# Attention with a gated expert layer: logits issued ahead of VectorE's reads of the scores, in 32-column tiles, and outputs transposed by halves

## The chip, the core and the metric

The kernel runs on one core of a Trainium2 chip. The metric is the device time of one execution in microseconds (us). Five engines work side by side, each through its own instructions in a fixed order: TensorE (PE in the profile; PEld is its loading of the stationary operand), VectorE (DVE), ScalarE (ACT), GpSimd (POOL) and SyncE (SP), which issues nearly all DMAs.

## The reference, cut to what matters

```python
# q, k, v: (4 batches, 8 heads, 768 positions, 64)
scores = q @ k.T / 8 - slope[head] * distance      # kept: first 8 keys, and the last 96 up to the query
a = softmax(scores over the kept keys)
x = (a @ v), heads side by side                    # 3072 tokens x 512
logits = x @ w_gate                                # 3072 x 8
e = argmax(logits); g = softmax(logits)[e]
# per expert: the 80 tokens with the largest g
out[tok] = g[tok] * (relu(x[tok] @ w1[e]) @ w2[e])  # w1: 512 x 1024, w2: 1024 x 512; all other rows 0
```

Everything is float32.

## The kernel before

The work is in three stages. **Attention** takes 24 blocks of 128 queries, each in two steps of four heads, so 48 steps u = 0 to 47; u // 2 is the block t. **Selection** ranks the tokens of every expert by their gate and makes lists of 80. **Experts** gathers the listed tokens and runs the two layers of eight experts, 512 KB of weights ("quarters") at a time.

In attention the order of work is the order in which the code is written (a manual schedule, all five engines), and each engine goes through its part of it in that order, waiting where it must. One step u issues:

- `transposes(u - 2, u - 5)`: TensorE turns the exponentials of step u - 2 (tiles `pwz`, two 64-row halves at a time, lines 152 and 161) and the attention output of step u - 5 (tile `x`, line 166: two full 128x128 transposes) into the PSUM tiles `tp0` and `tp1`; ScalarE copies `tp0` and VectorE `tp1` into the tile `ta` (lines 170 and 171);
- `scores(u)`: 12 TensorE products (24 records) into the PSUM tile `sc` (line 117; two buffers, two banks each), then four VectorE passes over `sc` that add the bias and find the row's extreme (line 124), each followed by a ScalarE exponential into `pwz` (line 128);
- `logits(u - 6)`: two products of the transposed output with the gate's weights `wgn` (line 215), written into spare columns of the same tile `sc`, and a small VectorE operation that takes them (lines 223 and 225);
- `norm(u - 1)`, and `weigh(u - 3)`: the products with the values `va` and `vb` into the PSUM tile `ub` (lines 187 and 197), and the division by the sum on VectorE (line 203), whose result is `x`; with the second half of a block `x` goes to DRAM;
- some steps of the routing of earlier blocks (`routes(3)`), and the loads of later blocks: SyncE issues q, keys and values four steps ahead, and every third step a quarter of the weights.

The two lines around which the change turns are, in `scores` and in the loop,

```python
                            out=ts[:, j, :w], in0=sc[:, hh, pp, :w], ...   # VectorE reads sc, four times
...
                scores(u)
                if 6 <= u:
                    logits(u - 6)          # TensorE writes the same tile sc
```

In this order TensorE may write the logits into `sc` only after VectorE's reads of `sc`.

After step 47, `DRAIN` lists what is left (t: transposes, l: logits, w: weigh, r and c: routing). Selection has `busy`, dummy products, between its rounds; `WARM` says how many. `NW` is the number of weight buffers in three pools.

Of the kernel before, what the change touches and what calls it, by code (L numbers as in the profile page):

```python
# [10 lines left out]
F32 = mybir.dt.float32  # L11
# [3 lines left out]
ALU = mybir.AluOpType  # L15
AX = mybir.AxisListType
# [14 lines left out]
CR = WH - CA  # L31
CAP = 80
KB = NG + P
NW = (24, 5, 1)
CL = 64

QUARTERS = [(k, e, c) for m in range(E + 1) for k, e in ((1, m), (2, m - 1)) if 0 <= e < E for c in range(4)]
GROUPS = (6, 6, 6, 4, 2)
# [8 lines left out]


DRAIN = (
    "t46,43 l42 w45 r r t47,44 l43 r w46 r r w47 t,45,46 r l44 r r l45 l46 t,47 r r r l47 c r r c r c r c r r c c r"  # L50
)
WARM = (6, 0, 6, 0, 6, 0, 6, 0, 9, 5)
FAR = 1.0e6
END = object()
SLOPES = [2.0 ** -(h + 1) for h in range(H)]
# [2 lines left out]
def fast_path(tc, a, out, cst, x_dram, inp):  # L58
    nc = tc.nc
    V, A, G, T = nc.vector, nc.scalar, nc.gpsimd, nc.tensor  # L60
    ident = cst["ident"]

    with ExitStack() as ctx:
# [20 lines left out]
        with tc.tile_pool(name="at_sb", bufs=2) as sp, tc.tile_pool(name="ps_a", bufs=1, space=PSUM) as psa, ExitStack() as pctx:  # L84

            pwz = [sp.tile([P, 4 * WH + P - CA], F32, name=f"pwz{i}", bufs=1) for i in range(3)]
            st = {}
# [8 lines left out]
            def scores(u):  # L96
                t, g = divmod(u, 2)
                m = TURN[t] % NB
                q, kt = inp.blk[t][0], inp.kts[TURN[t] // NB]
                nm, z, ts, pw = st[u]  # L100
                w = WH if m else P
                st["sc"] = psa.tile([P, 2, 512], F32, tag="sc", bufs=2, name=f"sc{u}")
                sc = st["sc"][:, :, :2 * WH].rearrange("p h (q k) -> p h q k", q=2)

                for pp in range(2):
                    pr = 2 * g + pp
                    for i in range(2):
                        c0 = KB * m - PREV + 64 * i if m else NG
                        for hh in range(2):
                            h = slice(64 * hh, 64 * hh + 64)  # L110

                            cuts = (0, w)
                            if m and i == hh:
                                cuts = (CR, w, 0, CR) if i == 0 else (CA, w, 0, CA)
                            o = 0
                            for c, e in zip(cuts[::2], cuts[1::2]):
                                T.matmul(  # L117
                                    sc[64 * i:64 * i + 64, hh, pp, o:o + e - c], q[h, pr * P + 64 * i:pr * P + 64 * i + 64],
                                    kt[h, pr, c0 + c:c0 + e], start=True, stop=True, skip_group_check=True)
                                o += e - c  # L120
                for hh in range(2):
                    for pp in range(2):
                        j = 2 * pp + hh
                        V.tensor_tensor_reduce(  # L124
                            out=ts[:, j, :w], in0=sc[:, hh, pp, :w], in1=cst["tab" if m else "tab0"][:, 2 * g + pp, hh, :], scale=-0.125,
                            scalar=3.0e38, op0=ALU.add, op1=ALU.min, accum_out=nm[:, j:j + 1],
                        )
                        A.activation(  # L128
                            out=pw[:, j, :w], in_=ts[:, j, :w], func=AF.Exp, bias=nm[:, j:j + 1], scale=-1.0, accum_out=z[:, j:j + 1],
                        )  # L130

            def norm(u):
                z = st[u][1]
# [3 lines left out]
            def transposes(u=None, *xs):  # L137
# [5 lines left out]
                ta = sp.tile([P, 2, 512], F32, tag="ta", name=f"ta{u}_{xs}")  # L143
                hs = [slice(64 * i, 64 * i + 64) for i in range(2)]
                n = 0
                if u is not None:
                    pw = pwz[u % 3]
                    for j in range(4):

                        o = j * WH + (CR if m and j % 2 else 0)  # L150
                        for i in range(2):
                            T.transpose(out=tps[i][:, 64 * j:64 * j + 64], in_=pw[hs[i], o:o + P], identity=ident[hs[i], hs[i]])
                    n = 256
                    st[u, "ta"] = ta
                    if m:
# [53 lines left out]
            def logits(u):  # L209

                t, g = divmod(u, 2)
                ps = st["sc"][:, 1, 2 * WH:2 * WH + E] if g else st["sc"][:, 1, 2 * WH + E:2 * WH + 2 * E]
                xt = st.pop((u, "xt"))
                for pp in range(2):
                    T.matmul(ps, xt[:, pp, :], cst["wgn"][:, 2 * g + pp, :E], start=pp == 0, stop=pp == 1, skip_group_check=True)
                k = next(i for i in range(len(GROUPS)) if t < sum(GROUPS[:i + 1]))
                n, t0 = GROUPS[k], sum(GROUPS[:k])
                if t == t0 and g == 0:
                    st["rt"] = Route(nc, sp, cst, t0, n)
                rt = st["rt"]  # L220
                lg = rt.lg[:, t - t0, :]
                if g == 0:
                    V.tensor_copy(out=lg, in_=ps)
                    return
                V.tensor_tensor(out=lg, in0=ps, in1=lg, op=ALU.add)
                st.pop((t, "x"))
                if n < 3:
                    rt.one(lg, t - t0)
                elif t == t0 + n - 1:
                    routing.append(rt.all())  # L230
                if t == t0 + n - 1 and t < NT - 1:
                    routing.append(rt.rest(lambda: st["sc"][:, 0, 2 * WH:2 * WH + E], cst["capm"]))

            def go(g, n):
                for _ in islice(g, n):
# [7 lines left out]
            routing = []  # L243
# [8 lines left out]
            for u in range(nu):  # L252
# [40 lines left out]

            for _ in islice(wipe, 4):
                pass
            st["sc"] = psa.tile([P, 2, 512], F32, tag="sc", bufs=2, name="rest")
            for k in DRAIN.split():
                if k == "r":
                    routes(1)
                elif k == "c":  # L300
                    go(choice, 1)
                elif k[0] == "t":
                    transposes(*(int(x) if x else None for x in k[1:].split(",")))
                elif k[0] == "w":
                    weigh(int(k[1:]))
                else:
                    logits(int(k[1:]))
                    if k == "l46":
# [6 lines left out]
            go(choice, 99)  # L315
            routes(99)
            assert not routing
            cn = st["sc"][:, 0, 2 * WH:2 * WH + E]
# [777 lines left out]
```

## Time and profile before

| | us |
|---|---|
| median of 3 runs (lowest to highest) | 446.76 (443.24 to 449.04) |
| the profiled execution, its own time | 450.29 |
| its span, first to last instruction | 448.5 |

Columns and terms: a row of a timeline gives the start and the length of an instruction or of a merged run (x24: 24 of them), the line of the kernel, the operation, and in brackets how long the engine had been idle before it and what ended that. Lengths of matmuls are modelled and overlap, so the pace is read from the starts. [...]

### The profile page before, as it was taken

What the parts mean: (1) busy time and instruction counts of PE and PEld (TensorE: products, weight loads), DVE (VectorE), ACT (ScalarE), POOL (GpSimd) and SP (SyncE); (2) the same over time, 40 slices, a digit from 0 to 9 for tenths busy, and PEclk for the clock granted to TensorE, in tenths of its full rate; (3) what the DMA queues carried; (4) which work ended last, traced back from release to release, by engine and by line L of the source; (5) the groups of instructions that cost most, each with busy time, mean ns of one, the idle gap of its engine ahead of it and who ended that gap; (6) DMA issues with size and microseconds to landing.
All of it is one profiled execution on the core that took longest, in us unless ns stands there. A gap on an engine that the chain in (4) does not pass through costs nothing. (4 is left out here: it accounts for less than half of the span.)

```text
span 448.5 us, 12361 instructions
## 1 busy us (share of the span) xinstructions
PE 373.6 (83%) x5149; PEld 275.2 (61%) x5149; DVE 156.2 (35%) x747; ACT 130.8 (29%) x476; POOL 54.6 (12%) x183
## 2 busy tenths in 40 slices
PE   3987877778788777787887877988987999999992
PEld 3766766667666666676666766776443455565551
DVE  5733333454443444434333335335551111001110
ACT  4734234343323334324234233221000211111110
POOL 4200111000002000000200000010207001111112
PEclk9955555555555656555555555555568999999997
DMA  7992135464212446423222430077995999960000
GB/s 208 315 344 78 37 102 162 140 213 140 70 60 89 153 140 213 138 91 109 77 90 91 137 119 26 24 260 288 359 359 144 345 330 364 387 245 25 18 18 24
DMA packets 37812, 73.24 MB, mean 163 GB/s; under 512 B 3476, under 2 KB 10516, under 8 KB 37748
## 3 DMA queue, kind: packets, MB, share of 16 engines
q1 hardware_dynamic: 36452, 69.74, 45.3%
q0 software_dynamic: 1152, 2.63, 1.9%
q8 instruction: 42, 0.69, 0.6%
q14 instruction: 22, 0.18, 0.1%
q10 hardware_dynamic: 144, 0.00, 0.0%
HBM read 58.46 MB, written 14.16 MB: 162 GB/s over the span
## 5 line engine op out<-in xcount | busy, mean ns | idle before, releaser
L128 ACT ACTIVATE pwz<-ts,nm 128x168 f32<-128x168 f32 (+1 forms) x192 | 80.0, 417 | 61.8 <-DVE nm L124 61.7
L117 PE MATMUL sc<-kt,q 64*64 64x104 f32 (+3 forms) x1088 | 65.2, 399 | 6.2 <-DVE kt L858 5.6
L117 PEld LDWEIGHTS sc<-kt,q 64*64 64x64 f32 x1088 | 52.2, 208 | 20.2 <-issue 18.4
L124 DVE CUSTOM_DVE_ANT_0 ts<-sc,tab 128x168 f32<-128x168 f32 (+1 forms) x192 | 51.0, 322 | 30.8 <-PE sc L117 30.7
L203 DVE TENSOR_TENSOR x<-ub,z 128x256 f32<-128x256 f32 x48 | 20.3, 423 | 60.7 <-PE ub L197 56.1
L569 PE MATMUL yp<-w,htm 128*32 128x256 f32 x512 | 39.7, 382 | 1.0 <-DVE vb L614 1.0
L134 POOL TENSOR_SCALAR z<-z 128x4 f32<-128x4 f32 x48 | 10.7, 222 | 241.5 <-ACT pwz L128 241.2
L128 ACT ACTIVATION_READ_ACCUMULATOR pwz<-ts,nm 128x1 f32 x192 | 35.8, 186 | 0.0
L569 PE MATMUL hm<-w,xt 128*32 128x512 f32 x256 | 34.6, 608 | 0.6 <-issue 0.6
L572 PE MATMUL yp<-w,htl 128*32 128x128 f32 x512 | 25.7, 273 | 0.0
L616 POOL DMA_INDIRECT out_dram<-vb,si x16 | 15.6, 975 | 82.4 <-ACT vb L613 39.1
L572 PEld LDWEIGHTS yp<-w,htl 128*32 128x32 f32 x512 | 16.7, 110 | 10.9
L572 PEld LDWEIGHTS hl<-w,xt 128*32 128x32 f32 x256 | 9.1, 112 | 19.2 <-issue 16.9
L572 PE MATMUL hl<-w,xt 128*32 128x256 f32 x256 | 20.7, 390 | 0.0
L585 DVE TENSOR_SCALAR va<-hl 128x256 f32<-128x256 f32 x8 | 3.4, 424 | 39.7 <-PE hl L572 39.7
L425 PE MATMUL lps<-svx,ones 128*128 128x480 bf16 x45 | 16.5, 531 | 0.0
L569 PEld LDWEIGHTS yp<-w,htm 128*32 128x32 f32 x512 | 14.2, 110 | 3.1 <-DVE vb L614 1.2
L124 DVE DVE_READ_ACCUMULATOR2_ANT nm<- 128x1 f32 x192 | 15.9, 83 | 0.0
L561 ACT COPY xt<-xf 128x320 f32<-128x320 f32 x8 | 3.4, 425 | 38.9 <-PE xf L560 32.6
L584 ACT ACTIVATE va<-hm 128x512 f32<-128x512 f32 x8 | 4.8, 597 | 28.5 <-PE hm L569 27.8
L595 DVE COPY htl<-tl 128x256 f32<-128x256 f32 x8 | 3.4, 425 | 26.9 <-PE tl L593 26.9
L614 DVE TENSOR_SCALAR vb<-yp,gs 128x128 f32<-128x128 f32 x8 | 2.8, 350 | 25.9 <-ACT vb L613 25.9
(1051 smaller groups left out, 678.4 us busy)
## 6 DMA issues: line engine op xcount, KB each, us to landing
w<-in_w_dram SPq DMA_DIRECT2D x64, 512.0 KB
x_dram<-x SPq DMA_DIRECT2D x24, 256.0 KB
out_dram<-zero SPq DMA_DIRECT2D x12, 512.0 KB
q<-in_q_dram SPq DMA_DIRECT2D x23, 256.0 KB
vb<-in_vb_dram SPq DMA_DIRECT2D x20, 256.0 KB
va<-in_va_dram SPq DMA_DIRECT2D x20, 208.0 KB
kt<-in_kT_dram SPq DMA_DIRECT2D x4, 816.0 KB
kt<-in_kT_dram SPq DMA_DIRECT2D x3, 544.0 KB
```

The costliest lines, as they stand in the source:

```text
L117: T.matmul(sc[64 * i:64 * i + 64, hh, pp, o:o + e - c], q[h, pr * P + 64 * i:pr * P + 64 * i + 64], kt[h, pr, c0 + c:c0 + e], start=True, ...
L124: V.tensor_tensor_reduce(out=ts[:, j, :w], in0=sc[:, hh, pp, :w], in1=cst["tab" if m else "tab0"][:, 2 * g + pp, hh, :], scale=-0.125, sca ...
L128: A.activation(out=pw[:, j, :w], in_=ts[:, j, :w], func=AF.Exp, bias=nm[:, j:j + 1], scale=-1.0, accum_out=z[:, j:j + 1],)
L134: G.tensor_scalar(out=z, in0=z, scalar1=1.0e-9, scalar2=None, op0=ALU.add)
L203: V.tensor_tensor(out=x[:, 256 * g:256 * g + 256].rearrange("p (q h d) -> p h q d", q=2, h=2), in0=up, in1=z.rearrange("p (q h) -> p h q", ...
L425: nc.tensor.matmul(ps[:, :480], cst["ones"], cst["svx"].rearrange("p s t -> p (s t)"), start=True, stop=True, skip_group_check=True)
L561: A.copy(out=xts[e % 2][:, :, :CAP], in_=xp)
L569: T.matmul(main[p, :n], x[:, 32 * g:32 * g + 32], w[:, n * i:n * i + n], start=first, stop=last, skip_group_check=True)
L572: T.matmul(rest[32 * i:32 * i + 32, :n], xl, w[:, n * i:n * i + n], start=first and rest.tensor is not main.tensor, stop=last, skip_group_ ...
L584: A.activation(out=hs[0], in_=hm, func=AF.Relu)
L585: V.tensor_scalar(out=hs[1], in0=hl[:, :256], scalar1=0.0, scalar2=None, op0=ALU.max)
L616: G.indirect_dma_start(out=out.rearrange("t (q d) -> (t q) d", d=n), out_offset=bass.IndirectOffsetOnAxis(ap=si[:, i, e:e + 1], axis=0), i ...
```

## The change

- `logits` is split by blocks. `logits1(t)`, in odd steps from u = 7, multiplies all of a block's transposed output with the gate's weights: four products, one for each 128 features, each with the 32 columns of `wgn` as the stationary operand, so that each writes 32 rows of its own (a 32-column tile of the array). `take1` copies the 128x128 result to SBUF (`ls`). In the next step `logits2(t)` transposes it back (128x128) and `take2` adds the four parts. Both TensorE parts stand between the score products and VectorE's passes over `sc`; the VectorE parts stand behind the passes.
- The output `x` is transposed in 64-row halves: four products with 64 moving columns for two with 128.
- `ta` has three buffers for two, `ls` is new; the first pool of weights has 23 buffers for 24; `busy` runs 5 products for 6 in four rounds; `DRAIN` is written anew, and its logits of blocks 22 and 23 (`last_logits`) use 64-row output halves.

```diff
-NW = (24, 5, 1)
+NW = (23, 5, 1)
-    "t46,43 l42 w45 r r t47,44 l43 r w46 r r w47 t,45,46 r l44 r r l45 l46 t,47 r r r l47 c r r c r c r c r r c c r"
+    "t46,43 k20 w45 r r t47,44 j21 w46 r r k21 w47 t,45,46 r r l44 l45 r t,47 r r l46 r r l47 c r r c r c r c r r c c r"
-WARM = (6, 0, 6, 0, 6, 0, 6, 0, 9, 5)
+WARM = (5, 0, 5, 0, 5, 0, 5, 0, 9, 5)
...
+                t1, t2 = (u - 7) // 2, (u - 8) // 2
+                if u % 2 and t1 >= 0:
+                    logits1(t1)
+                if u % 2 == 0 and t2 >= 0:
+                    logits2(t2)
                 for hh in range(2):
                     for pp in range(2):
...
+                if u % 2 and t1 >= 0:
+                    take1(t1)
+                if u % 2 == 0 and t2 >= 0:
+                    take2(t2)
...
-                    o = x % 2 * 256
-                    for i in range(2):
-                        T.transpose(
-                            out=tps[i][:, n:n + P], in_=st[x // 2, "x"][:, o + P * i:o + P * i + P], identity=ident)
-                    st[x, "xt"] = ta[:, :, n:n + P]
-                    n += P
+                    for pp in range(2):
+                        o = x % 2 * 256 + P * pp
+                        for i in range(2):
+                            T.transpose(
+                                out=tps[i][:, n:n + 64], in_=st[x // 2, "x"][hs[i], o:o + P], identity=ident[hs[i], hs[i]])
+                        st[x, pp] = ta[:, :, n:n + 64]
+                        n += 64
...
+            def logits1(t):
+
+                for pr in range(NP):
+                    T.matmul(
+                        st["sc"][32 * pr:32 * pr + 32, 0, 2 * WH:2 * WH + P], cst["wgn"][:, pr, :], st.pop((2 * t + pr // 2, pr % 2)),
+                        start=True, stop=True, skip_group_check=True)
+
+            def take1(t):
+                ls = st[t, "l"] = sp.tile([P, P], F32, tag="ls", name=f"ls{t}")
+                V.tensor_copy(out=ls, in_=st["sc"][:, 0, 2 * WH:2 * WH + P])
+
+            def logits2(t):
+                T.transpose(out=st["sc"][:, 1, 2 * WH:2 * WH + P], in_=st.pop((t, "l")), identity=ident)
+
+            def take2(t):
+                rt, i = route(t)
+                V.tensor_reduce(
+                    out=rt.lg[:, i, :], in_=st["sc"][:, 1, 2 * WH:2 * WH + P].rearrange("p (q k) -> p k q", q=NP)[:, :E, :], axis=AX.X,
+                    op=ALU.add)
...
-                if 6 <= u:
-                    logits(u - 6)
```

TensorE around the logits of step 36, before: the end of the scores (`sc36`), the logits with their wait for VectorE, the products with the values of step 33, the next transposes.

```order
L117 MATMUL sc36_2622<-kt1_106,q2_103 64x168 x2
L117 MATMUL sc36_2622<-kt1_106,q2_103 64x64
L117 MATMUL sc36_2622<-kt1_106,q2_103 64x104
L215 MATMUL sc36_2622<-wgn_87,ta33_(30,)_2533 128x8 [waits DVE_49]
L215 MATMUL sc36_2622<-wgn_87,ta33_(30,)_2533 128x8
L187 MATMUL ub_220<-va1_108,ta33_(30,)_2533 64x64 x8
L197 MATMUL ub_220<-vb1_113,ta33_(30,)_2533 64x64 x8
L152 MATMUL tp0_35_(32,)_2672<-ident_142,pwz2_219 128x64 [waits Activation_49]
```

The same place now, an even step: the transpose of `ls14` stands there and waits for VectorE, and so does the first product with the values.

```order
L117 MATMUL sc36_2711<-kt1_106,q2_103 64x168 x2
L117 MATMUL sc36_2711<-kt1_106,q2_103 64x64
L117 MATMUL sc36_2711<-kt1_106,q2_103 64x104
L231 MATMUL sc36_2711<-ident_142,ls14_2662 128x128 [waits DVE_49]
L197 MATMUL ub_220<-va1_108,ta33_(30,)_2615 64x64 [waits DVE_49]
L197 MATMUL ub_220<-va1_108,ta33_(30,)_2615 64x64 x7
L207 MATMUL ub_220<-vb1_113,ta33_(30,)_2615 64x64 x8
L161 MATMUL tp0_35_(32,)_2760<-ident_142,pwz2_219 128x64 [waits Activation_49]
```

And in the odd step 37 behind it: four products into 32 rows each, from two `ta` tiles, without a wait of their own.

```order
L117 MATMUL sc37_2784<-kt1_106,q2_103 64x64
L117 MATMUL sc37_2784<-kt1_106,q2_103 64x104
L222 MATMUL sc37_2784<-ta33_(30,)_2615,wgn_87 32x128 x2
L222 MATMUL sc37_2784<-ta34_(31,)_2689,wgn_87 32x128 x2
L197 MATMUL ub_220<-va2_109,ta34_(31,)_2689 64x64 [waits DMAHW2_49,DVE_49]
```

What moved: the write into `sc` no longer follows VectorE's reads of it; the wait that TensorE has there is now for things that VectorE did in the step before (`ls14` comes from step 35).

VectorE in step 34, before: behind the last pass over the scores (`nm34`), the small operation on the logits waits for TensorE.

```order
L124 ISA ts34_2478,nm34_2476<-sc34_2479,tab_88 128x168
L124 ISA nm34_2476 128x1
L223 COPY lg12_2210<-sc34_2479 128x8 [waits PE_49]
L135 RECIPROCAL z33_2404<-z33_2404 128x4 [waits Pool_49]
L203 TENSOR_TENSOR x15_2448<-ub_220,z31_2261 128x2x2x64 [waits DVE_49,PE_49]
```

And now, in step 34:

```order
L129 ISA ts34_2557,nm34_2555<-sc34_2558,tab_88 128x168
L129 ISA nm34_2555 128x1
L235 TENSOR_REDUCE lg12_2429<-sc34_2558 128x8
L144 RECIPROCAL z33_2483<-z33_2483 128x4 [waits Pool_49]
L213 TENSOR_TENSOR x15_2530<-ub_220,z31_2327 128x2x2x64 [waits PE_49]
```

The wait in the middle is gone, and with it the place where VectorE, between its passes and the division, stood for TensorE; the first pass of a step now waits for the logits part as well as for the scores.

The output's transposes ahead of step 36, before and now (`x15`; 64 moving columns and twice as many rows):

```order
L161 MATMUL tp0_34_(31,)_2600<-ident_142,pwz1_218 128x64
L161 MATMUL tp1_34_(31,)_2601<-ident_142,pwz1_218 128x64
L166 MATMUL tp0_34_(31,)_2600<-ident_142,x15_2448 128x128
L166 MATMUL tp1_34_(31,)_2601<-ident_142,x15_2448 128x128
L117 MATMUL sc36_2622<-kt1_106,q2_103 64x104 [waits DMAHW6_49]
```

```order
L170 MATMUL tp0_34_(31,)_2687<-ident_142,pwz1_218 128x64
L170 MATMUL tp1_34_(31,)_2688<-ident_142,pwz1_218 128x64
L176 MATMUL tp0_34_(31,)_2687<-ident_142,x15_2530 128x64
L176 MATMUL tp1_34_(31,)_2688<-ident_142,x15_2530 128x64
L176 MATMUL tp0_34_(31,)_2687<-ident_142,x15_2530 128x64
L176 MATMUL tp1_34_(31,)_2688<-ident_142,x15_2530 128x64
L117 MATMUL sc36_2711<-kt1_106,q2_103 64x104 [waits DMAHW6_49]
```

They now have the form of the transposes ahead of them. SyncE's queue and GpSimd's have the same instructions in the same order as before, but for the number of weight buffers.

## Rows read from the trace of the kernel before

**Rows 1.** The page's first two parts: busy time and share of the span, and TensorE's granted clock in 40 slices of the span (tenths).

```profile
PE 373.6 (83%) x5149; PEld 275.2 (61%) x5149; DVE 156.2 (35%) x747; ACT 130.8 (29%) x476; POOL 54.6 (12%) x183
...
PEclk9955555555555656555555555555568999999997
```

**Rows 2.** The view of waits: engine, what it was about to do and on which line, for whom it waited; us in total, times, longest.

```profile
PE sc L215 <- DVE nm L124: 51.0, 42, 1.3
...
DVE x L203 <- PE ub L197: 56.1, 39, 1.5
...
DVE ts L124 <- PE sc L117: 30.7, 45, 0.9
```

**Rows 3.** The timeline of TensorE through one step of attention (u = 14) and into the next.

```profile
93.71 1.02 PE L215 MATMUL sc<-wgn,ta_(11,)_1206 128*128 128x8 f32 x4 [1.23 <-DVE nm L124]
94.66 1.12 PE L187 MATMUL ub<-va,ta_(11,)_1206 104*64 104x64 f32 x16
95.72 0.71 PE L197 MATMUL ub<-vb,ta_(11,)_1206 64*64 64x64 f32 x16
96.35 0.36 PE L152 MATMUL tp_(13,)_1338<-ident,pwz 64*128 64x64 f32 x1
...
96.84 0.31 PE L161 MATMUL tp_(13,)_1338<-ident,pwz 64*128 64x64 f32 x1
...
96.94 0.31 PE L161 MATMUL tp_(13,)_1338<-ident,pwz 64*128 64x64 f32 x1
96.94 0.31 PE L161 MATMUL tp_(13,)_1339<-ident,pwz 64*128 64x64 f32 x1
97.19 0.48 PE L166 MATMUL tp_(13,)_1338<-ident,x 128*128 128x128 f32 x1
...
97.81 1.46 PE L117 MATMUL sc<-kt,q 64*64 64x104 f32 x24
100.49 1.02 PE L215 MATMUL sc<-wgn,ta_(12,)_1270 128*128 128x8 f32 x4 [1.23 <-DVE nm L124]
```

**Rows 4.** The timeline of VectorE in the same step: the copy of `tp1`, the first pass over the scores, and the read of the last pass's result.

```profile
97.91 0.69 DVE L171 COPY ta_(13,)_1340<-tp_(13,)_1339 128x512 f32<-128x512 f32 x1 [0.53 <-PE tp_(13,)_1339 L166]
99.33 0.33 DVE L124 CUSTOM_DVE_ANT_0 ts<-sc,tab 128x168 f32<-128x168 f32 x1 [0.73 <-PE sc L117]
...
100.35 0.08 DVE L124 DVE_READ_ACCUMULATOR2_ANT nm<- 128x1 f32 x1
```

**Rows 5.** The timeline of TensorE through the first steps, which have no logits yet.

```profile
17.03 0.27 PE L152 MATMUL tp_(0,)_441<-ident,pwz 64*128 64x64 f32 x1
...
17.91 0.87 PE L117 MATMUL sc<-kt,q 64*64 64x104 f32 x24
18.71 0.69 PE L187 MATMUL ub<-va,ta_()_382 104*64 104x64 f32 x16
19.32 0.46 PE L197 MATMUL ub<-vb,ta_()_382 64*64 64x64 f32 x16
19.72 0.27 PE L152 MATMUL tp_(1,)_508<-ident,pwz 64*128 64x64 f32 x1
```

**Rows 6.** Stretches of the span: length, busy time and count of PE, PEld, DVE, ACT and POOL, then TensorE's granted clock, the DMA share and GB/s.

```profile
16.26:20.67 4.41, 4.41 (x109) 3.44 (x101) 3.79 (x22) 3.70 (x16) 1.22 (x5) 1.00 1.06 309
20.67:23.42 2.75, 0.88 (x26) 0.70 (x25) 1.79 (x9) 1.68 (x8) 0.55 (x4) 0.94 1.08 343
...
165.56:170.24 4.68, 4.68 (x58) 3.92 (x58) 1.36 (x4) 1.59 (x7) 0.22 (x1) 0.54 0.26 76
170.24:173.30 3.06, 1.83 (x44) 1.68 (x46) 1.50 (x11) 1.78 (x8) 0.22 (x1) 0.99 0.90 282
173.30:293.10 119.80, 97.67 (x1290) 80.15 (x1287) 48.97 (x243) 41.59 (x159) 5.63 (x25) 0.50 0.29 97
```

**Rows 7.** Timelines of the experts' stage (TensorE, products on 32-column tiles) and of the end of attention (VectorE, a copy of 128x128 out of PSUM).

```profile
361.43 0.40 PE L572 MATMUL yp<-w,htl 128*32 128x128 f32 x8
361.65 0.61 PE L569 MATMUL yp<-w,htm 128*32 128x256 f32 x8
...
309.04 0.29 DVE L171 COPY taNone_(47,)_3557<-tp_None_(47,)_3556 128x128 f32<-128x128 f32 x1 [0.42 <-PE tp_None_(47,)_3556 L166]
```

**Rows 8.** The timeline of TensorE: the scores of step 6, the first with logits, and of step 47, the last.

```profile
21.24 0.87 PE L117 MATMUL sc<-kt,q 64*64 64x104 f32 x24 [0.56 <-DMA q<-in_q_dram]
...
290.87 1.13 PE L117 MATMUL sc<-kt,q 64*64 64x128 f32 x16
```

**Rows 9.** Stretches of attention, with the columns of rows 6.

```profile
21.24:33.00 11.76, 9.22 (x138) 7.82 (x140) 4.16 (x26) 4.38 (x18) 1.38 (x10) 0.58 1.03 347
33.00:293.10 260.10, 211.65 (x2814) 173.36 (x2813) 105.31 (x524) 92.81 (x358) 16.07 (x75) 0.52 0.33 110
```

**Rows 10.** The timelines of TensorE and VectorE in one round of selection: six dummy products, the counting products behind them, and VectorE's comparisons that these need.

```profile
320.86 2.58 PE L425 MATMUL lps<-svx,ones 128*128 128x480 bf16 x6
323.37 0.30 PE L466 MATMUL cnt<-oh,cm 128*31 128x8 bf16 x5
...
321.74 1.07 DVE L461 TENSOR_TENSOR cm<-left,kval 128x279 bf16<-128x279 f32 x3
```

More of the change, by code (lines that the diff above doesn't have):

```diff
@@ L142, in transposes @@
                 tps = [psa.tile([P, 512], F32, tag=f"tp{i}", name=f"tp{i}_{u}_{xs}") for i in range(2)]
-                ta = sp.tile([P, 2, 512], F32, tag="ta", name=f"ta{u}_{xs}")
+                ta = sp.tile([P, 2, 512], F32, tag="ta", bufs=3, name=f"ta{u}_{xs}")
                 hs = [slice(64 * i, 64 * i + 64) for i in range(2)]
@@ L207, in weigh @@
                     nc.sync.dma_start(out=x_dram[TURN[t] * P:(TURN[t] + 1) * P, :], in_=x)
-            def logits(u):
+            def logits1(t):
[6 more added lines that the diff above has]
+                V.tensor_copy(out=ls, in_=st["sc"][:, 0, 2 * WH:2 * WH + P])
@@ new lines, in logits2 @@
+            def logits2(t):
[5 more added lines that the diff above has]
+                    op=ALU.add)
+                if i == rt.n - 1:
+                    routing.append(rt.all())
+                    routing.append(rt.rest(lambda: st["sc"][:, 0, 512 - E:], cst["capm"]))
@@ L211, in logits, with route, last_logits @@
+            def route(t):
+                g = next(i for i in range(len(GROUPS)) if t < sum(GROUPS[:i + 1]))
+                i = t - sum(GROUPS[:g])
+                if i == 0 and (g, "rt") not in st:
+                    st["rt"] = st[g, "rt"] = Route(nc, sp, cst, t, GROUPS[g])
+                return st["rt"], i
+            def last_logits(u):
                 t, g = divmod(u, 2)
-                ps = st["sc"][:, 1, 2 * WH:2 * WH + E] if g else st["sc"][:, 1, 2 * WH + E:2 * WH + 2 * E]
-                xt = st.pop((u, "xt"))
+                ps = st["sc"][:, 0, E * g:E * g + E]
@@ L214, in logits @@
                 for pp in range(2):
[L215 to L221, printed above, removed]
+                    x = st.pop((u, pp))
@@ L222, in logits @@
+                    for i in range(2):
+                        T.matmul(
+                            ps[64 * i:64 * i + 64], x[:, i, :], cst["wgn"][:, 2 * g + pp, :E], start=pp == 0, stop=pp == 1,
+                            skip_group_check=True)
+                rt, i = route(t)
+                lg = rt.lg[:, i, :]
                 if g == 0:
                     V.tensor_copy(out=lg, in_=ps)
-                    return
-                V.tensor_tensor(out=lg, in0=ps, in1=lg, op=ALU.add)
-                st.pop((t, "x"))
@@ L227, in logits @@
[L227 to L232, printed above, removed]
+                else:
+                    V.tensor_tensor(out=lg, in0=ps, in1=lg, op=ALU.add)
+                    rt.one(lg, i)
             def go(g, n):
@@ L295, in fast_path @@
                 pass
-            st["sc"] = psa.tile([P, 2, 512], F32, tag="sc", bufs=2, name="rest")
             for k in DRAIN.split():
-                if k == "r":
+                f, n = k[0], k[1:]
+                if f in "jkl":
+                    st["sc"] = psa.tile([P, 2, 512], F32, tag="sc", bufs=2, name=f"sc{k}")
+                if f == "r":
                     routes(1)
-                elif k == "c":
+                elif f == "c":
                     go(choice, 1)
[L302 to L305, printed above, removed]
-                else:
-                    logits(int(k[1:]))
-                    if k == "l46":
+                elif f == "t":
+                    transposes(*(int(x) if x else None for x in n.split(",")))
+                elif f == "w":
+                    weigh(int(n))
+                elif f == "j":
+                    logits1(int(n))
+                    take1(int(n))
+                elif f == "k":
+                    logits2(int(n))
+                    take2(int(n))
+                else:
+                    last_logits(int(n))
+                    if int(n) == nu - 2:
                         rt = st["rt"]
@@ L317, in fast_path @@
             assert not routing
-            cn = st["sc"][:, 0, 2 * WH:2 * WH + E]
+            cn = st["sc"][:, 0, 512 - E:]
             count(nc, cn, [rt])
```

## The prediction

> **What bounds the kernel now.** The page comes first: TensorE is busy for 83% of the span, VectorE and ScalarE for about a third, and the granted clock stands at half for nearly all of attention, at its full level behind it [rows 1]. [...] The view of waits answers: TensorE's one large wait is for VectorE, 42 times ahead of the logits, 51.0 us in all [rows 2]. VectorE's own waits in attention are for TensorE, 56.1 us ahead of the division and 30.7 us ahead of the passes over the scores [rows 2]: it is early, not late. The timeline of one step shows the circle [rows 3, 4]. The scores go out at 97.81; VectorE starts its four passes at 99.33, when they are written, and ends at 100.43; TensorE, idle for 1.23 us, issues the logits at 100.49, with everything else of the step queued behind them in order. None of that queue (the products with the values, the next transposes) needs those passes. So TensorE's queue is the bound, plus one wait that only the order of writes to `sc` makes.
>
> One step of the usual kind takes 100.49 - 93.71 = 6.78 us: logits 0.95, products with the values 1.69, transposes 1.46, scores 1.45, wait 1.23 [rows 3]. From the scores of step 6 to those of step 47 it is 290.87 - 21.24 = 269.6 us for 41 steps, 6.58 each [rows 8] (blocks at the start of a batch are shorter).
>
> **The change, part by part.** *The wait.* With the logits ahead of the passes, TensorE goes from scores to logits to values without VectorE: 1.23 us a step less. What is late next? The new waits in that place (the transpose of `ls`, the first product with the values) are for VectorE's work of the step before; in VectorE's order the division stands ahead of the next copy and passes, and TensorE comes round to `ub` again only when those passes can start. I take 0 for them, and the whole 1.23 as the other bound (below, as a rival). The passes now start one logits part later, as do ScalarE's exponentials; these are next read two steps on, so 0 as well.
>
> *The logits.* Two steps cost 2 x 0.95 = 1.90 us now [rows 3]. The four products of the odd step are 8 records on four 32-column tiles with 128 moving columns; the row of that very form takes 361.65 - 361.43 = 0.22 us at the full clock [rows 7], so 0.44 at half, and with a change of form on either side (the gap from 96.94 to 97.19 is 0.14 longer than the 0.11 between two pairs [rows 3]) about 0.6. The even step's 128x128 transpose is half of the 0.62 from 97.19 to 97.81, about 0.35. That makes 0.5 a step, 0.45 less. Bounds: 0.22 (the product row alone) and 0.95 (as now).
>
> *The output's transposes.* From the last pair of 64-row transposes (96.94) to the scores (97.81) it is 0.87 us [rows 3]. Now two more pairs at the pairs' pace of 0.105 follow, and one change of form: 3 x 0.105 + 0.14 = 0.45. That is 0.42 less. The two halves of a pair start together, both at 96.94. [...]
>
> *VectorE and ScalarE.* `take1` is a 128x128 copy, 0.29 us [rows 7], `take2` a small sum; together about 0.15 a step more than the two small operations now, on an engine that has been busy for 105.31 us in 260.1 [rows 9], that is 2.67 us of a 6.58 us step (ScalarE: 92.81, 2.35). Hidden as long as a step is longer than about 2.8 us. Three buffers of `ta` only loosen.
>
> *Sum at half clock.* 1.23 + 0.45 + 0.42 = 2.10 us a step, so 6.58 - 2.10 = 4.5; 41 steps take 184 us for 269.6.
>
> *The clock.* It need not stay at half. Steps 3 to 5 have no logits and no wait: TensorE runs through without a gap, and its clock is at the full level [rows 5, 6]. There a step takes 19.72 - 17.03 = 2.69 us (transposes 0.88, scores 0.80, values 1.01), all with VectorE and ScalarE in the loop: what the new order looks like without the logits. It fell to half right behind the waits between 20.67 and 23.42, where only 0.88 of 2.75 us were busy, and in the stretch from 165.56 to 170.24, again 4.68 us without a gap, it rose, to fall within 3.1 us of the next wait [rows 6]. In the new order every step is such a stretch. So I expect it to be up most of the time. A step at the full level: 2.69, plus a logits part of 0.28 (the 0.22 and half a change of form), less half of the 0.42 for the transposes, 2.76 us. VectorE with 2.67 + 0.15 = 2.8 us a step is then level with TensorE; small waits of the two for each other come back, and with them spells at half clock. A fifth of the steps at 4.5 and the rest at 2.8 gives 3.1 on average: 41 x 3.1 = 127 us, 142 less.
>
> *DMA.* All that attention moves behind step 6 is 347 GB/s x 11.76 us + 110 x 260.1 = 32.7 MB [rows 9]; in 127 us that is 257 GB/s, where 347 was shown with the queues full, and at 2.8 us a step 285. Hidden, but no longer by much; the start of attention, where the queues are full up to 33 us, may cost a wait for a q tile of a microsecond or two, as the 0.56 us at 21.24 [rows 8].
>
> *The rest.* In selection, six dummy products take 2.51 us while VectorE is ready at 322.81, 0.56 before they end [rows 10]; one less saves 0.42 in each of up to four rounds. The first logits of the drain lose one wait of the 1.23 kind. Together 0 to 6 us, taken as 4. One weight buffer less costs nothing while weights come in ahead of the experts, whose stage keeps its pace. SyncE's order is unchanged.
>
> **The sum.** The profiled execution took 450.3 us, of which 269.6 are those 41 steps and 180.7 the rest. New: 180.7 - 4 + 127 = 304 us. It was 3.5 us above the median of the runs, so for the median I say 301.
>
> **The rivals.** *Half clock for most of attention.* The waits that come back, or the look of the new work (the lone 128x128 transpose, loads of weights between), could hold the clock down: for it speaks that several busy stretches of before, as in most of the 119.8 us behind 173.3, never raised it [rows 6]; against it, that each of those ended in a wait of 1.2 us, which is gone. All steps at 4.5: 180.7 - 4 + 184 = 361; half of them: 326.
>
> *The wait moves to the values.* The first product with the values now has a wait for VectorE of its own. Were the awaited work behind the passes, 1.23 us a step would return: 5.7 us at half clock, 41 x 5.7 = 234, and 410 us in all. Against it: what it must wait for (`ub` being read by the division of the step before) stands ahead of the passes.
>
> *Slower: the softmax chain is the loop's bound.* If scores, passes, exponentials and the transposes that read them set the pace and not TensorE's queue, the logits ahead of the passes add their 0.5 to 0.95 us to each of 41 steps, 20 to 39 us, and the kernel comes to 470 to 490. It decides if TensorE stands idle ahead of the transposes (line 152); the timeline has no wait there at all [rows 3], and the passes are read two steps later.
>
> **How the numbers follow.** Mostly full clock, 285 to 320: 0.55. Half clock in half of the steps or more, 320 to 366: 0.33. The wait moved: 0.08. Slower: 0.04. The likeliest gives 301; the range reaches from all steps at the full level (177 + 41 x 2.76 = 290, less the drain's upper bound and 3 for the median: 285) to all steps at half (361 and 3 for dearer logits: 364). About 2% is what a measurement of this kernel tells from no change: faster 0.95, same 0.01, slower 0.04.
>
> **What would show it.** In the profile after, no wait of TensorE ahead of the logits (51.0 us before); transposes to scores within 0.45 us of the last pair at half clock; a step of 2.8 us where the clock is full and 4.5 where it is half; PEclk at 8 or 9 through most of attention; VectorE busy for nearly the whole step; DMA near 250 GB/s. I am wrong if PEclk stays at 5, if a new wait of about a microsecond stands ahead of the values or the transposes, or if q or value loads come late step after step.

## The result and the profile after

| | before, us | after, us |
|---|---|---|
| median (lowest to highest) | 447.81 (443.24 to 449.04) | 295.03 (291.94 to 298.21) |
| the profiled execution, its span | 450.29, 448.5 | 298.21, 296.5 |

Without the two executions of after that were over 1.5% longer than its fastest (297.1 and the profiled 298.2 us), the ratio is 0.656, 95% interval 0.649 to 0.662. The page of after, where [rows 1] stood, with the DMA share in the same 40 slices:

```profile
PE 262.0 (88%) x5279; PEld 180.8 (61%) x5279; DVE 148.9 (50%) x747; ACT 126.7 (43%) x476; POOL 54.5 (18%) x183
...
PEclk9999799999999968999996557799999999999996
DMA  6999668995799946777299998799999993000000
```

PEclk is TensorE's granted clock in tenths of its full level (9 is 90% or more); in the tables of stretches it is a share, so that 1.00 is the full level and 0.50 half of it. Attention ends in slice 20, and the clock is at its full level nearly all the way there (0.96 over the 41 steps below). The view of waits, against [rows 2]: TensorE's 51.0 us ahead of the logits have no successor, and no other wait of TensorE for VectorE in attention is among the long ones. VectorE's waits for TensorE, before 86.8 us in [rows 2] and 45.7 more ahead of the small operations on the logits, are down to these and a few of at most 1.6 us:

```profile
DVE ts L129 <- PE sc L222: 10.1, 19, 1.3
...
DVE ts L129 <- PE sc L231: 5.4, 12, 1.1
...
DVE x L213 <- PE ub L207: 2.5, 3, 1.7
```

TensorE through one step (u = 19), against [rows 3] (by their tiles step 17 and the start of 18, not 14) and [rows 5]: scores, logits by blocks, values, transposes, scores, without a wait, in 62.76 - 59.96 = 2.80 us for 6.78.

```profile
59.96 0.87 PE L117 MATMUL sc<-kt,q 64*64 64x104 f32 x24
60.76 0.30 PE L222 MATMUL sc<-ta_(12,)_1301,wgn 128*32 128x128 f32 x2
...
61.12 0.69 PE L197 MATMUL ub<-va,ta_(13,)_1373 104*64 104x64 f32 x16
61.73 0.46 PE L207 MATMUL ub<-vb,ta_(13,)_1373 64*64 64x64 f32 x16
62.12 0.27 PE L161 MATMUL tp_(15,)_1520<-ident,pwz 64*128 64x64 f32 x1
...
62.76 0.38 PE L117 MATMUL sc<-kt,q 64*64 64x104 f32 x5
```

The next step, with the single 128x128 transpose for logits, takes 2.71 us. Stretches of attention, with the columns of [rows 6]: from the scores of step 6 to those of step 47 (what [rows 8] and [rows 9] bounded), a piece in the middle, and one of two spells at half clock:

```profile
20.62:146.86 126.24, 118.21 (x3034) 95.68 (x3030) 100.78 (x537) 93.03 (x376) 17.38 (x84) 0.96 0.76 251
...
51.30:96.50 45.20, 43.32 (x1151) 35.01 (x1148) 38.97 (x212) 35.68 (x146) 5.41 (x24) 1.00 0.86 283
...
31.20:34.60 3.40, 3.40 (x68) 2.58 (x62) 2.06 (x12) 1.83 (x8) 0.00 (x0) 0.50 0.84 307
```

The 41 steps take 126.2 us for 269.6. The rest of the execution is 298.2 - 126.2 = 172.0 us for 180.7. TensorE is idle for 8 us of the 126, and most of that is of a kind that before did not show: pauses in the midst of a group of like products, where the program has no wait at all ("issue": the engine waited for nothing that the profile shows). There are seven, 6.8 us in all; the two longest:

```profile
30.61 0.27 PE L176 MATMUL tp_(4,)_736<-ident,x 64*128 64x64 f32 x1 [1.31 <-issue]
...
104.48 0.45 PE L207 MATMUL ub<-vb,ta_(27,)_2383 64*64 64x64 f32 x12 [1.81 <-issue]
```

Behind each of these two the clock went to half, at 31.2 for 3.4 us and at 106.3 for 6.8; behind the five shorter ones (0.41 to 1.12) it did not.

### The profile page after: what moved, and what is told of

Read it like the earlier page. It is cut to its first block, busy times and chain, and to the rows that moved or that the text cites. A ratio compares the mean times of both kernels' runs of the same rounds, so it can differ in the third digit from the quotient of the medians.

```text
span 296.5 us, 12787 instructions
## 1 busy us (share of the span) xinstructions
PE 262.0 (88%) x5279; PEld 180.8 (61%) x5279; DVE 148.9 (50%) x747; ACT 126.7 (43%) x476; POOL 54.5 (18%) x183
## 5 line engine op out<-in xcount | busy, mean ns | idle before, releaser
L117 PE MATMUL sc<-kt,q 64*64 64x104 f32 (+3 forms) x1088 | 45.0, 290 | 7.8 <-DVE kt L897 5.6
L117 PEld LDWEIGHTS sc<-kt,q 64*64 64x64 f32 x1088 | 33.9, 143 | 11.6 <-issue 8.2
L213 DVE TENSOR_TENSOR x<-ub,z 128x256 f32<-128x256 f32 x48 | 19.3, 401 | 3.5 <-PE ub L207 2.5
L611 PEld LDWEIGHTS hl<-w,xt 128*32 128x32 f32 x256 | 8.4, 112 | 20.3 <-issue 17.8
L611 PE MATMUL hl<-w,xt 128*32 128x256 f32 x256 | 20.1, 387 | 0.0
L464 PE MATMUL lps<-svx,ones 128*128 128x480 bf16 x41 | 15.3, 533 | 0.0
```

The lines of the kernel that those rows point to most:

```text
L117: T.matmul(sc[64 * i:64 * i + 64, hh, pp, o:o + e - c], q[h, pr * P + 64 * i:pr * P + 64 * i + 64], kt[h, pr, c0 + c:c0 + e], start=True, ...
L213: V.tensor_tensor(out=x[:, 256 * g:256 * g + 256].rearrange("p (q h d) -> p h q d", q=2, h=2), in0=up, in1=z.rearrange("p (q h) -> p h q", ...
L464: nc.tensor.matmul(ps[:, :480], cst["ones"], cst["svx"].rearrange("p s t -> p (s t)"), start=True, stop=True, skip_group_check=True)
L611: T.matmul(rest[32 * i:32 * i + 32, :n], xl, w[:, n * i:n * i + n], start=first and rest.tensor is not main.tensor, stop=last, skip_group_ ...
```

## The experiments

The theory at the start: TensorE's one wait of 1.2 us a step was dear twice, by itself and because it held the clock at half; the order of the logits alone brings nearly everything. The rivals: the clock follows the form of the work, or it is low for a reason of its own.

**The old order with the new forms.**

```diff
...
-                if u % 2 and t1 >= 0:
-                    logits1(t1)
-                if u % 2 == 0 and t2 >= 0:
-                    logits2(t2)
                 for hh in range(2):
                     for pp in range(2):
...
+                if u % 2 and t1 >= 0:
+                    logits1(t1)
+                if u % 2 == 0 and t2 >= 0:
+                    logits2(t2)
                 if u % 2 and t1 >= 0:
                     take1(t1)
```

> The changed kernel with its logits parts put back behind VectorE's four passes; the new forms (32-column tiles, half transposes) stay. Theory (the waits of 1.2 us hold TensorE at half clock): the wait is back 42 times, 50 us in all, the clock falls to 0.5 for attention, a step is 4.5 + 1.2 = 5.7 us, attention from the scores of step 6 to those of step 47 takes some 235 us where it took 126, and the time is 405 to 420 us. Rival (the clock follows the work, the wait costs only itself): steps of 2.8 + 1.2 = 4.0 us at full clock, 345 us. Rival (the new forms did it): near 300 us.

Measured: 355.7 us, ratio 0.802 (0.795 to 0.810). The wait is back, 41 times 1.22 us, 50.3 us in all. But the clock stays up for two thirds of attention, on average 0.83. TensorE at full clock, then a stretch at half and one at full:

```profile
63.06 0.87 PE L117 MATMUL sc<-kt,q 64*64 64x104 f32 x24
65.14 0.30 PE L222 MATMUL sc<-ta_(8,)_1029,wgn 128*32 128x128 f32 x2 [1.22 <-DVE nm L124]
...
25.20:42.30 17.10, 14.01 (x233) 11.34 (x233) 7.19 (x34) 6.92 (x27) 1.85 (x12) 0.50 0.58 202
52.50:86.60 34.10, 23.45 (x621) 18.60 (x618) 22.52 (x115) 20.38 (x81) 4.04 (x17) 1.00 0.64 215
```

So half of the theory fell: with the same wait in every step the clock stayed full for 34.1 us. The time lies near the rival's 345. Its 41 steps of 4.0 us would be 164, the measured ones are 185.4: the spells at half clock, 65 us in all, with steps of some 5.8 us, make the difference. That the total is only 11 us above 345 is due to the rest of the kernel, 170 us for the 181 in the rival's sum.

**The order alone, old forms.**

(`products` is the TensorE half of the old `logits`, which keeps VectorE's half.)

```diff
+                if 6 <= u:
+                    products(u - 6)
                 for hh in range(2):
                     for pp in range(2):
...
                 if 6 <= u:
                     logits(u - 6)
```

> The kernel before with only the order changed: its two old logits products stand ahead of VectorE's passes, the small VectorE operation behind them; forms, buffers, dummies as before. Theory: no wait, clock full for most of attention, a step 2.7 + 0.5 for the logits, 3.2 to 3.3 us, 41 of them 133 us; 305 to 318 us. Rival (the new forms are needed to keep the clock up): half clock, step 6.58 - 1.23 = 5.35 us, 395 us.

Measured: 305.2 us (305.0 to 306.4), ratio 0.690 (0.684 to 0.695), at the lower end of what the theory said. The 41 steps take 131.6 us, at full clock from end to end, 3.23 us for the usual one (scores 0.80, logits 0.54, values 1.01, transposes 0.88):

```profile
21.48:153.06 131.58, 130.80 (x2932) 109.57 (x2932) 98.18 (x538) 91.32 (x370) 16.83 (x80) 1.00 0.73 241
```

**The wait kept, but filled with dummy products.**

```diff
+                    for _ in range(4):
+                        T.matmul(ub[:, 0, 4 * D:4 * D + P], ident, ident, start=True, stop=True, skip_group_check=True)
                     logits(u - 6)
```

> The kernel before in its old order, the wait for VectorE kept, but with four dummy 128x128 products into spare columns ahead of the logits, so that TensorE works while it would wait. Nothing that the result needs is changed. Theory (it is the idle stretch that lowers the clock): clock at the full level, the wait's stretch of 1.2 us remains as dummies, a step 4.2 to 4.4 us, 41 of them 175 to 180 us; 345 to 365 us, so that the clock is worth some 90 us and the wait by itself some 50. Rival (the clock is at half for another reason): the dummies take 2 us at half clock, 0.8 us more than the wait, and the time is 448 + 33 = 480 us.

Measured: 356.0 us, ratio 0.804 (0.797 to 0.811). The dummies fill the wait but for some 0.13 us a step, and the clock is full in all of attention:

```profile
44.46 1.16 PE L267 MATMUL ub<-ident 128*128 128x128 f32 x8
...
20.99:204.18 183.19, 178.14 (x3260) 149.09 (x3260) 106.61 (x539) 96.39 (x374) 17.71 (x85) 1.00 0.53 173
```

This is the cleanest split: the order, the forms and what TensorE has to wait for are those of before, and 90 us are gone only because TensorE did not stand still. From 269.6 to 183.2 us of attention is the clock, 86.4; from 183.2 to 131.6 (the order alone) is the wait's own time, 51.6.

**The dummies in twelve steps only.**

> The kernel before with the four dummy products in steps 6 to 17 alone; from step 18 on the wait of old. Theory (a clock that is up falls at the first waits of 1.2 us): full through steps 6 to 17 at 4.5 us each, half within a step or two behind, 6.6 us a step to the end; 448 - 12 x 2.1 = 423 us. Rival (which level holds depends on what was before: a clock that is up stays up with a wait of 1.2 us in 4.5): full for long stretches behind step 18 too, 370 to 400 us.

```diff
-                    for _ in range(4):
+                    for _ in range(4 if u < 18 else 0):
```

Measured, in one execution: 422.4 us, as the theory said. The first unfilled wait and what the clock did behind it:

```profile
75.14 0.61 PE L215 MATMUL sc<-wgn,ta_(12,)_1314 128*128 128x8 f32 x4 [1.22 <-DVE nm L124]
...
73.90:77.40 3.50, 2.28 (x51) 2.04 (x50) 1.93 (x13) 1.92 (x9) 0.22 (x1) 1.00 0.86 299
77.40:138.90 61.50, 50.65 (x658) 41.27 (x657) 24.46 (x121) 21.41 (x82) 3.88 (x17) 0.50 0.36 119
```

With the old forms, then, one wait of 1.22 us was enough, and the usual steps are at 6.78 us again from the second on; in attention the clock comes up once more, at 138.9 for 3.4 us. Twelve steps at full clock (1.00 up to 77.4 us) did not keep it up.

**The old order, with logits by blocks as the only new form.** To the edit of the first run here comes:

```diff
-                    for pp in range(2):
-                        o = x % 2 * 256 + P * pp
-                        for i in range(2):
-                            T.transpose(
-                                out=tps[i][:, n:n + 64], in_=st[x // 2, "x"][hs[i], o:o + P], identity=ident[hs[i], hs[i]])
+                    o = x % 2 * 256
+                    for i in range(2):
+                        T.transpose(out=tps[i][:, n:n + P], in_=st[x // 2, "x"][:, o + P * i:o + P * i + P], identity=ident)
...
```

> The changed kernel in the old order (logits parts behind the passes) and with full 128x128 transposes of the output, so that of the new forms only the logits by blocks are left. Theory (the new logits let the clock up in the old order, not the transposes): as with both forms, two thirds of attention at full clock, 360 to 365 us. Rival (the half transposes did it): half clock for most of attention, a step 4.9 + 1.2 = 6.1 us, 420 to 430 us.

Measured, in one execution: 361.1 us, as the theory said, clock 0.91 over the 41 steps, with the same wait ahead of the new logits:

```profile
75.23 0.30 PE L220 MATMUL sc<-ta_(12,)_1277,wgn 128*32 128x128 f32 x2 [1.22 <-DVE nm L124]
...
20.67:204.31 183.64, 135.08 (x2949) 102.58 (x2949) 109.58 (x536) 96.60 (x376) 17.60 (x85) 0.91 0.52 173
```

Full 128x128 transposes as before, a wait as before, and the clock is up for four fifths of the time. The changed kernel's lesser edits (buffers, dummies, drain) are in it too, but TensorE's steps show nothing of them: in its spells at half clock scores, wait, values and transposes take the 1.45, 1.23, 1.69 and 1.45 us of before. What differs in the step is what follows the wait: 0.54 us of 128x8 products before, 0.36 or 0.26 us of products with 128 moving columns now, at full clock. That the form of the logits decides whether this wait costs the clock is shown, by this one execution and the four with both new forms (0.91 and 0.83, for 0.52 before behind 33 us [rows 9]); by what measure it does so is not.

**Full transposes in the changed kernel.**

> The changed kernel with the output transposed as before, by two full 128x128 transposes for two pairs of 64-row halves. Theory: the transposes part is 0.2 us longer at full clock, but VectorE is level with TensorE, so between 0 and 9 us come through: 295 to 304 us, at the middle 299. Rival (loads of the halves follow each other): the halves are the dearer form, and the time is 286 to 295 us.

(The edit is the one above.) Measured: 295.2 us (294.4 to 302.4), ratio 0.666 (0.662 to 0.671); the changed kernel has 0.656 (0.649 to 0.662) above and 0.666 (0.662 to 0.670) when it was run again (below). No clear difference. Yet TensorE's steps do differ: transposes 0.88 us here and 0.64 there, a step 3.00 and 2.76 on average of the two kinds. The 41 steps:

```profile
21.12:147.12 126.00, 122.24 (x2949) 94.84 (x2949) 100.66 (x536) 92.14 (x372) 17.59 (x85) 1.00 0.77 253
```

126.0 us, where the changed kernel has 126.2 in one profile and 122.9 in a second. The halves make 41 x 0.24 = 9.8 us less work for TensorE, and most or all of it goes into pauses and half-clock spells: here there are four pauses, 2.9 us, and no such spell; in the changed kernel seven, 6.8 us, and when run again ten, 7.5 us. So VectorE, which the expectation named, is not what keeps the gain back: TensorE waits for it for 1.0 us in all of the 41 steps. Nor are the halves the dearer form, as the rival had it: they take 0.24 us a step less. The other form, logits by blocks, and the lesser edits bring the 10 us from the order alone, 305.2, to here.

**The pauses: no weights loaded during attention.**

```diff
-                if u % 3 == 2:
-                    next(ahead, None)
```

> The changed kernel without the loads of expert weights during attention: the 16 quarters that went out every third step are issued behind the drain. Theory (TensorE's pauses of 0.8 to 1.8 us in the midst of a group of products, with no engine to wait for, are its instructions coming late behind full DMA queues): with 8 MB less to move in attention there is at most one such pause, no half-clock spell behind it, and the 41 steps take 112 to 116 us for 126; what it brings in the total depends on whether the weights are there when the experts start: 284 to 296 us. Rival (the pauses follow the number of instructions per us alone): as many pauses, 41 steps in 124 to 128 us, 293 to 300 us.

Measured: 291.0 us (288.0 to 297.7), ratio 0.655 (0.648 to 0.662). TensorE's instructions are the same in the same order, and of the pauses one of 0.22 us is left; the 41 steps take 114.2 us at full clock. The total is not told apart from the changed kernel's 0.656 (0.649 to 0.662), and lies 4 us below it run again. Part of the gain is given back ahead of the experts, where the gathered rows now wait behind the late weights (1.44 us in the changed kernel):

```profile
19.62:133.78 114.16, 111.88 (x3035) 91.52 (x3031) 99.43 (x537) 92.69 (x376) 17.44 (x85) 1.00 0.67 212
...
176.21 0.77 PE L597 MATMUL xf<-ident,q 80*128 80x80 f32 x4 [4.33 <-DMA q<-x_dram,gi]
```

So the pauses hang on the load of the DMA queues, 212 GB/s here and 251 in the changed kernel. In attention 126.2 - 114.2 = 12.0 us go with it in the first profile of the changed kernel, and 122.9 - 114.2 = 8.7 us in the second. The pauses are 6.8 us in the first and 7.5 in the second; the 10.2 us at half clock, which the first alone has, cost some 4 us, by the difference of the two: (126.2 - 6.8) - (122.9 - 7.5).

**The same kernel again, half of the weights, and fewer dummies.** These three ran side by side.

> The changed kernel itself once more, beside the two that follow: 292 to 298 us. If TensorE's pauses come from its instructions arriving late behind the queues of DMA, they need not stand at the same steps as in the first profile; if they come from something in the order of the program, they do.

> The changed kernel with a quarter of the weights every sixth step for every third: 4 MB less to move in attention, and less left to load behind it than in the run without any. Theory (late instructions behind full DMA queues): pauses in between, 41 steps in 117 to 122 us, and the wait for the gathered rows ahead of the experts shorter than 4.3 us: 286 to 293 us, 4 below the changed kernel. Rival (pauses are no matter of the DMA load): no difference, 292 to 298 us.

> As the run with half the weights, and with 3, 3, 3 and 2 dummy products in the rounds of selection for 5. Theory (the dummies run at half clock, 0.42 us each, and end behind the point where VectorE has the first third of the comparison ready): 0.6 us less in each of four rounds, 2.5 us in all, the clock at half there as before and up again at the ranking: 284 to 291 us. Rival (the fewer dummies keep the clock at half for longer, into the experts): 3 us more.

```diff
-                if u % 3 == 2:
+                if u % 6 == 5:
-WARM = (5, 0, 5, 0, 5, 0, 5, 0, 9, 5)
+WARM = (3, 0, 3, 0, 3, 0, 2, 0, 9, 5)      # the last run only
```

Measured: 294.7 (ratio 0.666, 0.662 to 0.670), 293.3 (0.659, 0.655 to 0.664) and 291.6 us (0.655, 0.650 to 0.660). In the kernel run again the seven pauses stand at the same products as in the first profile, if not all with the same length, and there are three more; the clock is full throughout attention:

```profile
103.46 0.45 PE L207 MATMUL ub<-vb,ta_(27,)_2383 64*64 64x64 f32 x12 [1.83 <-issue]
```

So the places go with the program (seven of seven again), and whether a pause shows there goes with the DMA load (one, of 0.22 us, with the late weights). Half of the weights shorten the 41 steps only to 121.1 us, with four pauses of 4.3 us left, and with 3.7 us of waiting for the gathered rows: 1.4 us less in all, in the rival's range, too little to be sure of. With fewer dummies on top, the first three rounds of selection take 2.97, 2.67 and 2.69 us for 3.24 to 3.26, and all four are 2.3 us shorter for 2.5 expected; this version, with both edits, beats the changed kernel beside it by 1.7% (the intervals don't meet), though at 291.6 us it just misses the 284 to 291 expected. One of its rounds, where three dummies for five stand ahead of the counting products:

```profile
157.74 1.38 PE L464 MATMUL lps<-svx,ones 128*128 128x480 bf16 x3
...
159.12 0.95 PE L505 MATMUL cnt<-oh,cm 128*31 128x8 bf16 x24
```

**More dummies, to keep selection at full clock.** A try in the other direction.

```diff
-WARM = (5, 0, 5, 0, 5, 0, 5, 0, 9, 5)
+WARM = (8, 0, 8, 0, 8, 0, 6, 0, 4, 9, 5)
-            busy(nc, cst, scratch[:, 0], 4)
+            busy(nc, cst, scratch[:, 0], 9)
...
```

(The third edit, not shown, makes the place ahead of the ranking where the 4 new dummies run.)

> The changed kernel with more dummy products in selection, so many that at full clock they reach to where VectorE is ready: 9 for 4 behind the drain, 8, 8, 8, 6 for 5 in the rounds, 4 new ones ahead of the ranking. Theory (idle stretches lowered the clock at 157.5): selection stays at full clock, a round takes 2.5 us for 3.25, the products for the lists go at twice the pace, 5 us in all: 290 us. Rival (the clock falls there all the same): 8 dummies at 0.42 us make a round of 4.5 us, 5 us more in all: 300 us.

Measured: 292.6 us (292.4 to 294.1), ratio 0.659 (0.653 to 0.665), not told apart from the changed kernel. Both theories are in the trace: the clock fell at 158.2, behind gaps of 0.25 to 0.56 us between small products with 8 columns, rose at 165.0, and a round takes 165.58 - 161.12 = 4.46 us at half, then 168.40 - 165.58 = 2.82 at full, for 3.25:

```profile
161.12 3.38 PE L464 MATMUL lps<-svx,ones 128*128 128x480 bf16 x8
...
165.58 1.79 PE L464 MATMUL lps<-svx,ones 128*128 128x480 bf16 x8
...
168.40 1.39 PE L464 MATMUL lps<-svx,ones 128*128 128x480 bf16 x6
```

## Why the prediction was right, and where it was not

The time, 301 for 295.0, and the account of the 269.6 us of attention held: an order of writes, not the work, kept TensorE waiting, and the wait cost both itself (51.6 us) and the clock (86.4 us). By its steps:

- **The wait.** 1.23 us a step and nothing in its place: right. There is no wait ahead of the values or of the transpose of `ls`; by itself the wait was worth 51.6 us.
- **The logits.** 0.36 in odd and 0.26 in even steps at full clock, 0.31 for the 0.28 predicted; at half (in the old order with new forms) 0.59 and 0.41 for 0.6 and 0.35.
- **The transposes.** At half clock 1.05 us for 1.45, 0.40 less for the 0.42 predicted; at full 0.24 less for 0.21. The two transposes of a pair start together (in step 19 at 62.54 and 62.55, then both at 62.61), and the whole part takes 0.64 us with the halves, 0.88 without.
- **The step.** 2.76 us at full clock: 2.71 and 2.80 measured. The mean over the 41, 3.1 predicted and 3.08 measured, was **right by two errors that cancel.** The sum put a fifth of the steps at half clock, behind small waits of TensorE and VectorE for each other. Those waits were harmless: some three steps fell to half, behind pauses, and none in the second profile. The place of that loss was taken by the pauses. That the mean came out is luck.
- **DMA.** 251 GB/s for "near 250" predicted; that it stays **hidden is the step that failed.** The data came in time, with no wait for a q tile at step 6. But TensorE paused seven times, 6.8 us in all, and with the weights loaded late one pause of 0.22 us was left: 12.0 us went with that load in the first profile, 8.7 in the second. The prediction had no row for it: at 6.58 us a step before, the packets of kind "instruction" ended 4.2 us or more ahead of the products at these places (last section).
- **VectorE level with TensorE.** Busy for 100.8 us of 126.2, 2.46 a step for 2.8 predicted, in the stretch without half clock 39.0 of 45.2: **mis-sized.** Added up one by one, VectorE's operations of the 41 steps are 137.9 us long for 136.2 before, but they overlap more. It is close behind TensorE, but where the pauses are gone TensorE is busy for 111.9 of 114.2 us: TensorE's queue remains the bound.
- **The rest,** 4 us less predicted, 0 to 6, measured 8.7: **mis-sized.** The rounds gave 1.6 as reckoned. But the drain runs at full clock too and lost half of its time, from the scores of step 47 to the first dummy 9.8 us for 19.1; the term had one wait for it. The end behind the experts' last product gave 2.5 back.

```profile
290.87:310.01 19.14, 16.61 (x168) 14.60 (x167) 7.03 (x31) 4.29 (x16) 2.06 (x9) 0.50 0.71 255
```

```profile
146.86:156.66 9.80, 8.62 (x203) 6.73 (x199) 7.07 (x33) 3.99 (x15) 2.25 (x10) 1.00 1.01 351
```

(The drain of before, then of after.)

- **The reason given against half clock,** that each busy stretch of before "ended in a wait of 1.2 us, which is gone", was half a reason. With the old forms, filling the wait raised the clock (1.00 over the 41 steps), and one wait of 1.22 us lowered it (0.50 from 77.4 to 138.9); with the new logits the same wait left it up for four fifths or two thirds of attention. Had the order not changed, this kernel would have gained 90 us by its new forms, nearly all of it by that of the logits (361.1 us with that alone), and my 405 to 420 us for that case was wrong by 50.

None of the prediction's rivals came about: no long half clock, no wait at the values, no bound by the softmax chain.

## What to carry to other kernels

One wait of TensorE, 1.23 of a step's 6.78 us (18%), cost nearly a third of this kernel's time, 138 of 450 us (269.6 against 131.6 us of attention), 86 of them because the clock stood at half with it and at full level once the wait was filled; so look first at the granted clock of a stage, then at the one wait in its step, and ask whether the order of two writes to one tile makes it. Where the wait had to stay, products that nobody needs were worth 90 us here. And when TensorE's step had gone from 6.58 to 3.08 us, pauses of 6.8 us came up that before did not show, and 0.22 us of them was left without prefetches: look for them before the next saving on TensorE (here the half transposes, 9.8 us), which can be given back there.

## What the runs showed of the hardware

**Pauses on a grid, behind packets of kind "instruction".** The page has these packets as a DMA queue of their own:

```profile
q8 instruction: 43, 0.70, 1.0%
```

43 packets of 16 KB (0.70 MB), one about every 5.2 us through attention after and every 12 us before, so they follow TensorE's pace. Counted in the order of the trace, the seven pauses stand behind products 346, 474, 984, 1367, 2132, 2259 and 3153: every distance is a whole multiple of 127.6, within one. With full transposes, hence other products at these places, they are 474, 601, 1366 and 2132, on the same grid. A product and its weight load are two instructions (5279 of each on the page), so 127.6 products are 255 instructions; the 43 packets for all 10558 make one for 246, nearly the same.

That TensorE's instructions come in these packets, and that a pause is a packet coming late, is my reading; the profile does not show what a packet holds. Its times fit. Each place of the grid in attention has its packet, and no product there starts less than 1.28 us behind the end of it. Each of the seven pauses ends 1.3 to 1.6 us behind that end: the packet ahead of product 2259, for one, ran from 102.02 to 103.15, and the product started at 104.48. Before, the packet had ended 4.2 us or more ahead of the product at every place of the grid in attention. A packet takes as long with the weights loaded late (1.1 us on average either way), but starts earlier: 1.2 us on average behind the product at the previous place of the grid, for 2.1 in the changed kernel. Around the pause at 104.48 the 16 DMA engines were busy throughout (the share, before the rate in GB/s, is 1.03), with the columns of [rows 6]:

```profile
101.00:104.50 3.50, 1.69 (x50) 1.15 (x44) 2.24 (x12) 2.49 (x11) 0.44 (x2) 1.00 1.03 354
```

When a packet was asked for, the profile does not show either.

**The clock and what follows a wait.** The same 1.22 us of idleness a step went with half clock at once (old logits: 0.50 from 77.4 on, the wait at 75.14), with full clock for four fifths of the time (logits by blocks, full transposes: 0.91 on average) and for two thirds (both new forms: 0.83). Pauses of 0.84 and 1.12 us in work without other gaps left it up, those of 1.31 and 1.81 were followed by half clock, and those of 1.30 and 1.83 at the same two places in the second profile of the same kernel were not. It stays open what of a stretch decides.
